# Attention with routed experts on one core: the stretch ahead of the experts reordered, the router placed by two clocks, the second product in row form, four experts' rows turned by VectorE via DRAM

## The chip, the cores and the metric

The kernel runs on one core of one Trainium2 chip. A core has TensorE (PE, matrix products; PEld is its loading of stationary operands), VectorE (DVE), ScalarE (ACT), GpSimd (POOL) and SyncE (SP, which issues DMAs), each with an instruction stream of its own, executed in order, and 16 DMA engines. The metric is the device time of one execution in microseconds (us). It is compared by the median of several runs.

## What is computed

An attention with a sigmoid instead of a softmax, 8 batches of 12 heads, 448 positions, 64 values per head, all in fp32. Its output is read as 3584 tokens of 768 values. Each token goes to exactly one of 8 experts, 448 tokens per expert, assigned greedily by the largest logit over all pairs of token and expert. An expert is a two-layer product with a ReLU between.

```python
scores = scale * np.matmul(q, k.transpose(0, 1, 3, 2)) - np.log(S)
attn = 1.0 / (1.0 + np.exp(-scores))          # x = attn @ v, as (3584, 768)
logits = x @ w_gate                            # (3584, 8)
for idx in np.argsort(-logits.flatten()):      # greedy, with a capacity
    tok, e = idx // E, idx % E
    if assigned[tok] >= 0 or counts[e] >= cap: continue
    assigned[tok] = e; counts[e] += 1
for e in range(E):
    h = np.maximum(x[assigned == e] @ w1[e], 0.0)   # 448x768 @ 768x1024
    out[assigned == e] = h @ w2[e]                  # 448x1024 @ 1024x768
```

## The kernel before

**Precision.** A product of two fp32 operands is made of three products of a faster format: each operand is split into a high part (a rounded copy) and a low part (the difference), and high x high, high x low and low x high are summed in PSUM. For a weight tile `wr`, ACT writes the high part `wh` (L596) and POOL, now and then DVE, the low part `wl` (L598).

**Attention** (about the first 276 us) goes over 48 pairs of heads: `turn`, `scores`, `rest_scores`, `av`. `av` leaves the result transposed, in `XT[b]` with the 768 values along the partitions: a copy by DVE (L469) and, for every second pair, an addition (L471). `logits` (L476) multiplies `XT` by the gate weights; for the last batch it is cut in two, the first four pairs ahead of the last `av` and two behind it.

**Rows to DRAM.** `rows` (L486) turns a block of 112 tokens of `XT` on PE (six transposes, L490), copies it from PSUM with ACT (L492) into one of four buffers `xr`, and SP writes it to `xs` in DRAM (L493). There are 32 such blocks. They are left to the stretch between attention and the experts, mixed into the first search: two after each of its steps.

**The router.** For k = 0 to 7, `phase(k)` finds the expert that fills up next and its list of 448 tokens: `keys` (DVE), `search` (16 steps of two bits of a threshold; each step counts with three DVE instructions, L173), `pick`, `place`, `lists`. In phase 0 the sum over partitions of each step is a small PE matmul (L185); in later phases it is done by DVE alone with 32x32 transposes (L189, L195). `pick`, `place` and `lists` go through PE several times (L224, L252, L257, L284, L291). Each `yield` hands control back with the time, in ns, after which the next piece shall be emitted.

**The experts.** Rows of x are gathered by the list with an indirect DMA of POOL (`gather`, L618), turned on PE (`xturn`: three transposes per half block, L632; ACT takes the high part, L635, DVE the low part, L636). The first product has 4 x 36 matmuls of 448 columns, weights stationary (L680 to L684), into tiles of two PSUM banks. ReLU and split follow (L688 to L692). The second product has 3 x 48 matmuls of 448 columns, weights stationary again (L715 to L719), so its result lies transposed: ACT copies it to `yt` (L723), and `untranspose` turns it back on PE, 12 chores of two transposes per expert (L645), copied by ACT (L650). An indirect DMA of POOL writes the rows to their tokens (L653).

**What sets the order.** The whole program is one hand-made order. `moe` yields after every matmul with an assumed cost (`MM = 189` ns), which drives `clock`. When the clock passes `t_route`, the next piece of the router is emitted, and its yield plus `SLACK` sets the next time. `chores` holds (due time, last expert, piece): gathers, turns, result transposes; one per `CHORE_NS`. At the end of an expert, `flush` emits what the next one still needs, and as long as its list isn't there, the router is run on. `stream` issues weight loads three units ahead (SP, four buffers) and their splits two ahead. The simulated clock only sets the order in the streams; the engines then run as their semaphores let them.

```python
if t >= t_route:
    t_route = t + next(route, 0) + SLACK
```

Of the kernel before, what the change touches and what calls it, by code (L numbers as in the profile page):

```python
# [21 lines left out]
XR_BUFS = 12  # L22
XT_BUFS = 8
XA_BUFS = 4
AT_BUFS = 8
YT_BUFS = 3
LATE_PER_STEP = 2
LATE_KEYS = 2
T_KEYS, T_KE, T_STEP, T_DVE, T_KAP, T_PICK, T_TOT, T_OH, T_BT = 3600, 2100, 2050, 2025, 500, 2600, 600, 3800, 600
SLACK = 150  # L30
# [4 lines left out]
W_DVE = 84  # L35
# [78 lines left out]
class Router:  # L114
# [42 lines left out]
    def search(self, pe):  # L157
# [10 lines left out]
        for st in range(16):  # L168
# [11 lines left out]
            if pe:  # L180
                if nX is not None:
                    nc.vector.tensor_scalar(nX, K.kk[:, st + 1], JP, None, OP.bitwise_xor)
                yield T_STEP
# [30 lines left out]
            if not pe:  # L214
                yield T_DVE
# [31 lines left out]
    def place(self):  # L247
# [7 lines left out]
        yield T_TOT  # L255
# [10 lines left out]
    def lists(self):  # L266
# [6 lines left out]
        rr = wk.tile([112, 32], I16, name="r_rr")  # L273
# [6 lines left out]
        yield T_OH  # L280
# [7 lines left out]
        yield T_BT  # L288
# [30 lines left out]
    def phase(self, k):  # L319
        if k:  # L320
            self.remove()
        if k < 7:
            self.keys()
            yield T_KEYS
            yield from self.search(k == 0)
            yield T_KAP
            self.pick()
        else:
            self.left()
        yield T_PICK  # L330
        yield from self.place()
        yield from self.lists()


def moe_attention(tc, q, k, v, w_gate, w1, w2, out):
# [7 lines left out]
    with contextlib.ExitStack() as ctx:  # L343
# [8 lines left out]
        ld = actx.enter_context(tc.tile_pool(name="ld", bufs=2))  # L352
        wk = actx.enter_context(tc.tile_pool(name="wk", bufs=2))
        xa = actx.enter_context(tc.tile_pool(name="xa", bufs=1))

# [96 lines left out]
        def av(b, pr):  # L452
# [16 lines left out]
            nc.vector.tensor_copy(XT[b][:, pr, :], p[:, :S])  # L469
# [16 lines left out]
        def rows(b, c):  # L486
            xr = xa.tile([CP, DM], F32, name="xr", bufs=XA_BUFS)
# [13 lines left out]
        for i in range(NPR + 1):  # L501
# [32 lines left out]
        ps_t = ctx.enter_context(tc.tile_pool(name="ps_t", bufs=2, space=PSUM))  # L534
        ps_s = ctx.enter_context(tc.tile_pool(name="ps_s", bufs=2, space=PSUM))
        ps_a = ctx.enter_context(tc.tile_pool(name="ps_a", bufs=2, space=PSUM))
        R = Router(tc, K, cp, rw, ps_a)
# [4 lines left out]
        def routing():  # L542
            for kx in range(E):
# [6 lines left out]
                yield 0  # L550
# [11 lines left out]
        actx.close()  # L562

# [4 lines left out]
        units = [(kx, st, i, j) for kx in range(E) for st, n in ((0, 4), (1, 3)) for i in range(n) for j in range(2)]  # L568
# [4 lines left out]
        def load_w(u, behind=False):  # L573
# [5 lines left out]
            t = wp.tile([128, 1024], F32, name="wr")  # L579
            if behind:  # L580
                nc.gpsimd.memset(t[:1, :1], 0.0)
            if st == 0:
                t = t[:, :768].rearrange("p (a f) -> p a f", a=3)
                src = w1[ds(gate[kx], 1)].rearrange("e (a p) f -> p (e a) f", p=128)
                nc.sync.dma_start(t, src[:, 3 * j:3 * j + 3, i * 256:(i + 1) * 256])
            else:
                t = t.rearrange("p (a f) -> p a f", a=4)
                src = w2[ds(gate[kx], 1)].rearrange("e (a p) f -> p (e a) f", p=128)
                nc.sync.dma_start(t, src[:, 4 * j:4 * j + 4, i * 256:(i + 1) * 256])
            raw[u] = t  # L590

        def split_w(u):
            n = 3 if units[u][1] == 0 else 4
            hi = wp.tile([128, 1024], F32R, name="wh")[:, :n * 256].rearrange("p (a f) -> p a f", a=n)
            lo = wp.tile([128, 1024], F32R, name="wl")[:, :n * 256].rearrange("p (a f) -> p a f", a=n)
# [14 lines left out]
        xg, XH = {}, {}  # L610

# [8 lines left out]

        def xturn(kx, j, n, hf, wide):
# [3 lines left out]
            xh, xl = XH[kx]  # L625
            if wide and hf:
# [12 lines left out]
        MM = 189  # L639

        def untranspose(kx, yr, i, yt, j, n, t0=0, end=False):

            p = R.bank() if end and j % 2 else ps_t.tile([128, 512], F32, name="tp")
            for d2 in range(2):
# [171 lines left out]
```

## Time and profile before

| | us |
|---|---|
| median of 3 runs | 891.27 (888.68 to 891.42) |
| the profiled execution | 887.23 |
| its span, first to last instruction | 885.5 |
| attention | 0 to about 276 |
| rows, first search, first list, first turn | about 276 to 335 |
| eight experts | 335 to 877 |
| last writes | 877 to 885.5 |

Times in the views below are microseconds from the span's start. In the chain of waits a row is start, length and what the end of the program hung on there; "issue" means that the engine waited for nothing the profile shows. In the groups a row gives line, engine, operation, out<-in, shape and type, count, then busy time and mean ns of one, then the engine's idle time ahead of it and what ended it. Matmuls are pipelined: the length of one is a latency, and what one costs in a row of them is the distance of their starts. A busy PE is thus not a PE at its peak.

### The profile page before, as it was taken

How to read it: one execution, taken by the hardware profiler on the slowest of the kernel's cores; microseconds unless marked ns; L12 is line 12 of the kernel's file. 1: busy time of each engine (PE TensorE's matmuls, PEld its weight loads, DVE VectorE, ACT ScalarE, POOL GpSimd, SP SyncE). 2: the span in 40 equal slices, each digit the busy share in tenths (PEclk: the TensorE clock that was granted, in tenths of full speed). 3: DMA queues.
4: the chain of work that ended last, by engine and by line, in shares of the span. 5: the costliest groups of instructions: out<-in, count | busy, mean ns of one | idle time of the engine just before them, and what ended most of it. 6: DMA issues, size and time to landing. Idle time of an engine off the chain costs nothing.

```text
span 885.5 us, 16232 instructions
## 1 busy us (share of the span) xinstructions
PE 837.8 (95%) x5507; PEld 639.0 (72%) x5507; DVE 531.4 (60%) x2047; ACT 456.2 (52%) x610; POOL 467.4 (53%) x449
## 2 busy tenths in 40 slices
PE   6999999999998729998999999999999999999996
PEld 3455455455555518987988988988888888889996
DVE  4665555555554778958869779779689521421110
ACT  6777777777774724434424424434434434443431
POOL 9645444444400014846864964873883882752651
PEclk9999999999999969999999999999999999999999
DMA  9876666665603945434443542452552542632511
GB/s 172 168 144 127 132 125 123 131 126 120 138 12 100 299 161 153 136 107 161 136 133 117 146 156 75 157 164 95 153 164 70 178 146 72 228 111 72 192 49 63
DMA packets 203507, 117.57 MB, mean 133 GB/s; under 512 B 143936, under 2 KB 193088, under 8 KB 203424
## 3 DMA queue, kind: packets, MB, share of 16 engines
q1 hardware_dynamic: 190688, 83.03, 36.0%
q0 software_dynamic: 10880, 33.28, 11.9%
q8 instruction: 43, 0.70, 0.3%
q10 hardware_dynamic: 1856, 0.23, 0.2%
q14 instruction: 40, 0.33, 0.1%
HBM read 94.47 MB, written 22.02 MB: 132 GB/s over the span
## 4 chain that ended last, share of the span: by engine, by line
PE 77%; DVE 8%; DMA 5%; issue 4%; POOL 3%; ACT 1%; SPq 1%; POOLq 0%; ACTq 0%; DVEq 0%
PE tp L461 13%; PE sc L437 11%; PE sc L682 8%; PE sc L680 8%; PE sc L684 8%; PE sc L717 6%; PE sc L719 6%; PE sc L715 6%; PE tp L467 2%; DMA xs<-xr 2%; DVE r_junk L173 2%; PE sc L447 2%; PE tp L645 2%; DMA xr<-xs,r_idx 2%; PE tp L632 2%
## 5 line engine op out<-in xcount | busy, mean ns | idle before, releaser
L598 POOL TENSOR_TENSOR wl<-wr,wh 128x768 fp32r<-128x768 f32 (+1 forms) x96 | 205.9, 2155 | 134.6 <-ACT wh L596 126.9
L427 ACT ACTIVATE at<-sc,bias 128x896 f32<-128x896 f32 x168 | 161.0, 1006 | 63.1 <-PE sc L447 38.2
L372 POOL DMA_DIRECT2D nkq<-in_q_dram x188 | 118.6, 646 | 111.5 <-DVE kqT L412 104.7
L719 PE MATMUL sc<-hh,wl 128*128 128x448 f32 (+2 forms) x400 | 151.4, 378 | 0.0
L717 PE MATMUL sc<-hl,wh 128*128 128x448 f32 (+2 forms) x400 | 145.4, 364 | 0.1
L684 PE MATMUL sc<-xh,wl 128*128 128x448 f32 (+2 forms) x396 | 145.4, 367 | 0.0
L682 PE MATMUL sc<-xl,wh 128*128 128x448 f32 (+2 forms) x396 | 144.9, 366 | 0.0
L715 PE MATMUL sc<-hh,wh 128*128 128x448 f32 (+2 forms) x400 | 143.9, 360 | 0.0
L680 PE MATMUL sc<-xh,wh 128*128 128x448 f32 (+2 forms) x396 | 143.8, 363 | 0.0
L173 DVE TENSOR_SCALAR_CACHE_REDUCE r_junk<-r_KE,r_T 128x224 bf16<-128x224 f32 x315 | 123.2, 441 | 0.1
L461 PE MATMUL tp<-at,nv 128*64 128x448 f32 x576 | 118.8, 548 | 0.0
L596 ACT ACTIVATE wh<-wr 128x768 fp32r<-128x768 f32 (+1 forms) x112 | 102.0, 939 | 13.2 <-DMA wr<-in_moe_w_dram 13.1
L692 POOL TENSOR_TENSOR hl<-yt,hh 128x896 fp32r<-128x896 f32 x32 | 68.3, 2136 | 44.5 <-ACT yt L691 41.8
L421 DVE TENSOR_TENSOR kqL<-kqT,kqH 128x896 fp32r<-128x896 f32 (+1 forms) x49 | 52.6, 1073 | 58.3 <-ACT kqH L419 58.2
L688 ACT ACTIVATE hh<-sc 128x896 fp32r<-128x896 f32 x32 | 29.5, 920 | 111.0 <-PE sc L684 111.0
L618 POOL DMA_INDIRECT xr<-xs,r_idx x32 | 32.0, 1002 | 97.5 <-ACT wh L596 86.7
L717 PEld LDWEIGHTS sc<-hl,wh 128*128 128x128 f32 x400 | 75.2, 188 | 7.0 <-issue 1.1
L598 DVE TENSOR_TENSOR wl<-wr,wh 128x768 fp32r<-128x768 f32 (+1 forms) x16 | 25.1, 1571 | 91.7 <-ACT wh L596 91.5
L461 PEld LDWEIGHTS tp<-at,nv 128*64 128x64 f32 x576 | 37.1, 136 | 59.1 <-issue 57.9
L682 PEld LDWEIGHTS sc<-xl,wh 128*128 128x128 f32 x396 | 74.5, 188 | 6.3 <-issue 0.5
L715 PEld LDWEIGHTS sc<-hh,wh 128*128 128x128 f32 x400 | 75.6, 189 | 4.4
L680 PEld LDWEIGHTS sc<-xh,wh 128*128 128x128 f32 x396 | 74.7, 189 | 5.5
(156 smaller groups left out, 1323.7 us busy)
## 6 DMA issues: line engine op xcount, KB each, us to landing
wr<-in_moe_w_dram SPq DMA_DIRECT2D x64, 384.0 KB
wr<-in_moe_w_dram SPq DMA_DIRECT2D x48, 512.0 KB
xs<-xr SPq DMA_DIRECT2D x32, 336.0 KB
nkq<-in_k_dram SPq DMA_DIRECT2D x190, 56.0 KB
nkq<-in_q_dram POOLq DMA_DIRECT2D x188, 56.0 KB, 2.6
nv<-in_v_dram SPq DMA_DIRECT2D x92, 96.0 KB
nr<-in_v_dram SPq DMA_DIRECT2D x46, 32.0 KB
xr<-xs,r_idx POOLq DMA_INDIRECT x32, 4.4
```

What stands on the lines that cost most here:

```text
L173: nc.vector.tensor_scalar(junk, KE, T[:, i:i + 1].bitcast(F32), None, OP.is_ge, OP.add, accum_out=cnt[:, i:i + 1])
L372: qn.dma_start(t[o:o + 32, n], rws[x])
L427: nc.scalar.activation(a, p[:, :, :S], AF.Sigmoid, bias=bias, scale=1 / math.sqrt(D))
L461: nc.tensor.matmul(p[j * 64:j * 64 + 64, :S], nat["v", b, g][:, h0 + j, c, :], AT[b, pr, c][:, j, :], start=(c == 0), stop=(c == 2 and pr ...
L596: nc.scalar.activation(hi, raw[u], AF.Copy)
L598: eng.tensor_tensor(lo, raw[u], hi.bitcast(F32), OP.subtract)
L680: nc.tensor.matmul(ph[:, f, lo:hi], wh[:, a, fs], xh[:, dd, lo:hi], start=st, stop=False)
L682: nc.tensor.matmul(ph[:, f, lo:hi], wh[:, a, fs], xl[:, dd, lo:hi], start=False, stop=False)
L684: nc.tensor.matmul(ph[:, f, lo:hi], wl[:, a, fs], xh[:, dd, lo:hi], start=False, stop=en)
L715: nc.tensor.matmul(py[:, d2, :w], wh[:, a, dsl], h1, start=st, stop=False)
L717: nc.tensor.matmul(py[:, d2, :w], wh[:, a, dsl], h2, start=False, stop=False)
L719: nc.tensor.matmul(py[:, d2, :w], wl[:, a, dsl], h1, start=False, stop=(j == 1 and a == 3))
```

## The change

1. *Stretch ahead of the experts.* The last batch's logits run in one piece behind the last `av`; the copy of that last product goes to ACT, beside DVE's addition. No row block stands ahead of the router's start any more, three follow it ahead of the first search, then two per step as before. The pools of attention are released first, so that the row blocks get eight buffers (`xo`) and three PSUM tiles instead of four and two.
2. *Router by two clocks.* Pieces yield (cost on DVE, whether the next piece needs PE). A second clock `dve` sums DVE's costs, those of the turns of x included; a piece that begins on PE is emitted 150 ns after it, another 400 ns ahead of it. All costs are new, a matmul of the first product counts 206 ns and one of the second 175, and turns and routing matmuls are added to the PE clock. From phase 1 on, an index tile of `lists` lies in PSUM instead of SBUF.
3. *Second product in row form.* Tokens are stationary (128 columns of h, high or low), the weights move, 384 columns at a time: 2 halves x 8 slices x (3 + 3 + 3 + 2) = 176 matmuls per expert, whose result has tokens along the partitions. The last block has 64 tokens: its high and low parts lie side by side as one stationary operand, and the two halves of the result are added (ACT copies and a POOL addition; DVE for the very last). `untranspose` is gone; ACT copies the result straight into `yr`. Weight units of the second product become 8 of 768 values per partition instead of 6 of 1024. The ReLU is written in two parts.
4. *Turn by DVE via DRAM for experts 4 to 7.* After the gather, SP writes the rows to a DRAM buffer `xq` (`stage`) and reads them back with four DMAs per pair of blocks (`fetch`) so that 32x32 block transposes by DVE into PSUM (`vturn`) complete the turn, with the 768 values spread over the partitions in another order. The first weights of these experts are loaded in the matching order, with four DMAs of 32 partitions per unit instead of one.

```diff
@@ search, lists, phase
-            if not pe:
-                yield T_DVE
+            if not pe and st < 15:
+                yield T_STEP if st else T_STEP0, False
...
-        rr = wk.tile([112, 32], I16, name="r_rr")
+        rr = wk.tile([112, 32], I16, name="r_rr") if alone else P[:, 320:352]
...
@@ av, rows and the stretch ahead
-            nc.vector.tensor_copy(XT[b][:, pr, :], p[:, :S])
+            (nc.scalar.copy if (b, pr) == (B - 1, NP - 1) else nc.vector.tensor_copy)(XT[b][:, pr, :], p[:, :S])
...
-            xr = xa.tile([CP, DM], F32, name="xr", bufs=XA_BUFS)
+            xr = xo.tile([CP, DM], F32, name="xr", bufs=XO_BUFS)
...
-            if old == (B - 1, NP - 2):
-                bg.append(lambda: logits(B - 1, range(NP - 2)))
...
-        logits(B - 1, [NP - 2, NP - 1])
-        late.pop(0)()
+        logits(B - 1, range(NP))
...
+        lctx.close()
         ps_a = ctx.enter_context(tc.tile_pool(name="ps_a", bufs=2, space=PSUM))
+        xo = actx.enter_context(tc.tile_pool(name="xo", bufs=1))
+        ps_s = actx.enter_context(tc.tile_pool(name="ps_w", bufs=3, space=PSUM))
         R = Router(tc, K, cp, rw, ps_a)
         R.start(LE)
         late.pop(0)()
...
@@ load_w
+                else:
+                    src = w1[ds(gate[kx], 1)].rearrange("e (g a p) f -> g p (e a) f", g=4, a=ND)
+                    for g in range(4):
+                        nc.sync.dma_start(t[32 * g:32 * g + 32], src[g, :, 3 * j:3 * j + 3, fs])
...
+        def stage(kx, j, n):
+            nc.sync.dma_start(xq[kx % 2][j * 128:j * 128 + n], xg[kx, j][:n])
+
+        def fetch(kx, j0, j1):
+            t = xg[kx, 4 + j0] = xp.tile([128, 8, DM // 4], F32, name="xw", bufs=2)
+            v = xq[kx % 2].rearrange("(j c) (g w) -> g c j w", c=32, g=4)
+            for g in range(4):
+                nc.sync.dma_start(t[32 * g:32 * g + 32, :j1 - j0], v[g, :, j0:j1])
+
+        def vturn(kx, j, n, hf):
...
+            dve[0] = max(dve[0], clock[0]) + T_VTURN
...
+            for a in range(3):
+                nc.vector.transpose(p[:, a * n:(a + 1) * n].rearrange("p (j w) -> p j w", w=32),
+                                    w[:, :, (3 * hf + a) * 32:(3 * hf + a + 1) * 32])
...
+            nc.scalar.activation(xh[sl], pv, AF.Copy)
+            nc.vector.tensor_tensor(xl[sl], pv, xh[sl].bitcast(F32), OP.subtract)
...
@@ moe: ReLU and second product
+                parts = ((h[:, :, 0], h[:, :, 1], slice(0, W2)), (r[:, :, :64], r[:, :, 64:], slice(W2, S)))
+                for h1, h2, t in parts:
+                    nc.scalar.activation(h1, ph[:, :, t], AF.Relu)
...
+            for i in range(2):
+                cs = slice(i * W2, (i + 1) * W2)
+                py = [ps_s.tile([128, 2, 512], F32, name="sc") for _ in range(2)]
+                for j in range(4):
...
+                    for z in range(2):
+                        for a in range(2):
...
+                            for c in range(2):
+                                o = py[z][:, c, :W2]
+                                if z == 0 or c == 0:
+                                    t = slice((2 * z + c) * 128, (2 * z + c + 1) * 128)
+                                    terms = ((h[:, 0, t], wh), (h[:, 1, t], wh), (h[:, 0, t], wl))
+                                else:
+                                    terms = ((r, wh), (r, wl))
+                                for n, (hs, w) in enumerate(terms):
+                                    nc.tensor.matmul(o, hs, w[:, a], start=st and n == 0,
+                                                     stop=en and n == len(terms) - 1)
+                                    yield MM2
...
@@ prepare and the loop
-                lag = max(5000, min(14000, start + 40000 - t0))
+                lag = max(6500, min(17000, start + 50000 - t0))
...
+                if kx + 1 >= BY_DVE:
+                    for j, n in blocks():
+                        t = t0 + 1500 * j + T_LAND
+                        chores.append((t, kx + 1, lambda j=j, n=n: stage(kx + 1, j, n)))
+                        if j % 2:
...
+                            chores.append((t + T_BACK2, kx + 1, lambda r=r: fetch(kx + 1, *r)))
...
-                    t_route = t + next(route, 0) + SLACK
+                    cost, hop = next(route, (0, False))
+                    dve[0] = max(dve[0], t) + cost
+                    clock[0] += T_PE if hopped[0] else 0
+                    hopped[0] = hop
+                    t_route = dve[0] + (T_HOP if hop else T_FEED)
```

The new costs, in ns: `T_KEYS` 4850, `T_STEP0` 3300, `T_STEP` 2340, `T_KAP` 350, `T_PICK` 3000, `T_TOT` 700, `T_OH` 4900, `T_BT` 1500, `T_XL` 560, `T_TURN` 420, `T_PE` 250, `T_LAND` 8000, `T_BACK2` 4000, `T_READ` 5000, `T_VTURN` 1200. `W_DVE` goes from 84 to 96 with the finer units: both mean expert 6, from which on DVE makes every second `wl`.

More of the change, by code (lines that the diff above doesn't have):

```diff
@@ L34 @@
 FIRST = 4000.0
-W_DVE = 84
+BY_DVE = 4
+T_LAND, T_BACK2, T_READ, T_VTURN = 8000, 4000, 5000, 1200
+W_DVE = 96
 class Consts:
@@ L264, in place, with lists @@
         self.sl = sl
-    def lists(self):
+    def lists(self, alone):
         nc, K, wk, sl = self.nc, self.K, self.wk, self.sl
@@ L329, in phase @@
             self.left()
-        yield T_PICK
+        yield T_PICK, True
         yield from self.place()
-        yield from self.lists()
+        yield from self.lists(k == 0)
 def moe_attention(tc, q, k, v, w_gate, w1, w2, out):
@@ L562, in moe_attention @@
         actx.close()
+        ps_t = ctx.enter_context(tc.tile_pool(name="ps_t", bufs=2, space=PSUM))
+        ps_s = ctx.enter_context(tc.tile_pool(name="ps_s", bufs=2, space=PSUM))
         wp = ctx.enter_context(tc.tile_pool(name="wp", bufs=4))
@@ L566, in moe_attention @@
         xp = ctx.enter_context(tc.tile_pool(name="xp", bufs=1))
-        units = [(kx, st, i, j) for kx in range(E) for st, n in ((0, 4), (1, 3)) for i in range(n) for j in range(2)]
+        units = [(kx, st, i, j) for kx in range(E) for st, n in ((0, 4), (1, 2)) for i in range(n) for j in range(8 // n)]
         NU = len(units) // E
@@ L578, in load_w @@
                 gate[kx] = nc.sync.value_load(picked[kx][:1, :1], min_val=0, max_val=E - 1)
-            t = wp.tile([128, 1024], F32, name="wr")
+            t = wp.tile([128, 768], F32, name="wr")
             if behind:
@@ L610, in moe_attention @@
         xg, XH = {}, {}
+        xq = [dr.tile([S, DM], F32, name=f"xq{i}") for i in range(2)]
         def blocks():
@@ L625, in xturn @@
             xh, xl = XH[kx]
+            if not wide:
+                clock[0] += T_TURN
+            dve[0] = max(dve[0], clock[0] + 900) + T_XL
             if wide and hf:
@@ L638, in moe_attention, with scatter @@
         scat, chores = [], []
[L639 to L644, printed above, removed]
-                nc.tensor.transpose(p[:n, d2 * 128:(d2 + 1) * 128], yt[:, d2, j * 128 - t0:j * 128 - t0 + n], ident)
-            dst = yr[j][:n, i * 256:(i + 1) * 256]
-            if end and j % 2:
-                nc.vector.tensor_copy(dst, p[:n, :256])
-            else:
-                nc.scalar.copy(dst, p[:n, :256])
-            if i == 2:
-                nc.gpsimd.memset(spacer, 0.0)
-                ins = nc.gpsimd.indirect_dma_start(
-                    out=out, out_offset=bass.IndirectOffsetOnAxis(ap=listed[kx][:n, j:j + 1], axis=0),
-                    in_=yr[j][:n], in_offset=None)
-                for o in scat:
-                    tc.declare_no_dep(ins.ins, o.ins, reason="rows of other tokens")
-                scat.append(ins)
+        MM, MM2, W2 = 206, 175, 384
+        def scatter(kx, yr, j, n):
+            nc.gpsimd.memset(spacer, 0.0)
+            ins = nc.gpsimd.indirect_dma_start(
+                out=out, out_offset=bass.IndirectOffsetOnAxis(ap=listed[kx][:n, j:j + 1], axis=0),
+                in_=yr[j // 2][:n, j % 2], in_offset=None)
+            for o in scat:
+                tc.declare_no_dep(ins.ins, o.ins, reason="rows of other tokens")
+            scat.append(ins)
         def moe(kx):
@@ L666, in moe @@
                 cuts = ((0, 256), (256, S)) if kx + i == 0 else ((0, S),)
-                mm = 107 if len(cuts) > 1 else MM
+                mm = 117 if len(cuts) > 1 else MM
                 for lo, hi in cuts:
@@ L730, in moe_attention @@
+        clock, dve = [0.0], [FIRST]
         while 0 not in listed:
```

147 lines of the change are left out of this document (79 added, 68 removed).

## The prediction

> **What bounds the kernel now.** I read the page's busy line first, then windows by stage, then the chain of waits between attention and the experts, then the timeline of TensorE (PE) among the experts.
>
> ```profile
> PE 837.8 (95%) x5507; PEld 639.0 (72%) x5507; DVE 531.4 (60%) x2047; ACT 456.2 (52%) x610; POOL 467.4 (53%) x449
> ```
>
> ```profile
> 301.00:305.00 4.00, 3.17 (x26) 2.33 (x23) 2.85 (x19) 2.17 (x3) 0.00 (x0) 1.00 0.95 299
> 581.70:643.60 61.90, 61.60 (x350) 54.00 (x350) 50.15 (x264) 25.43 (x41) 41.07 (x29) 1.00 0.41 131
> ```
>
> A window gives its length, then the busy time of PE, PEld, DVE, ACT and POOL, the granted clock, DMA share and GB/s. Among the experts (second window, from one routing list to the next) PE is full at clock 1.00, and DVE has 11.75 us free. So what is taken off PE there is worth its slot, and nothing else is, as long as DVE keeps up. Ahead of the experts PE isn't full; there the chain decides:
>
> ```profile
> 269.58 0.90 PE tp L482 x32
> 275.18 0.59 PE tp L482 x16
> 277.55 0.66 PE rt L134 x2
> 282.86 0.52 DVE r_junk L173 x3
> 300.67 4.42 DMA xs<-xr
> 306.99 0.81 ACT xr L492
> 315.01 0.18 PE rt L185
> 316.85 0.18 PE rt L185
> 317.51 0.17 DVE r_kap L217
> ```
>
> The chain there is the first routing search: 282.86 to 317.51, 34.65 us for 16 steps, while an unhindered step takes 316.85 - 315.01 = 1.84. The search's small matmuls (L185) queue in PE behind row transposes, those behind ACT's copies into xr, and those behind the write that frees a buffer (300.67). The experts' first matmuls follow at a fixed distance: pick, list, gather, turn of x.
>
> **The stretch ahead.** The logits at 269.58 leave their place between the last two products, so all behind them starts 0.90 earlier. The copy of the last product goes to ACT and runs beside DVE's addition instead of ahead of it: up to 0.7 more. All six pairs' logits then start at 275.18 - 1.6 = 273.6 and take at most 0.90 + 0.59 = 1.5; 0.4 for the sum into LE brings R.start to 275.5. It starts at 277.55 today, behind a row: -2.0. *The search*: eight row buffers instead of four, three PSUM tiles instead of two. Two rows a step cost ACT 2 x 0.81, less than 1.84, and PE isn't full even today (3.17 of 4.00). The writes need 32 x 344 KB / 299 GB/s = 36.8 us, from 277 to about 314: a row comes every 0.93 us and leaves every 1.15, so the backlog reaches eight only near the end. I take 30.5 for the 16 steps (the first is longer): -4.2, together **-6.2**. Bounds: -2 if the writes gate the steps as today, -7.5 if every step takes 1.84. The gather comes some 10 us after the search, with the writes done either way.
>
> **The matmuls of the experts.** Spacing by width, and what an interruption costs (timeline; start, length, instruction):
>
> ```profile
> 346.26 0.37 PE L682 MATMUL sc<-xl,wh 128*128 128x448 f32 x1
> ...
> 367.94 0.37 PE L715 MATMUL sc<-hh,wh 128*128 128x448 f32 x1
> 336.25 0.28 PE L682 MATMUL sc<-xl,wh 128*128 128x256 f32 x1
> ...
> 337.44 0.28 PE L684 MATMUL sc<-xh,wl 128*128 128x256 f32 x1
> 409.73 0.36 PE L682 MATMUL sc<-xl,wh 128*128 128x448 f32 x1
> 409.94 0.38 PE L645 MATMUL tp<-ident,yt 128*128 128x128 f32 x2
> 410.07 0.45 PE L684 MATMUL sc<-xh,wl 128*128 128x448 f32 x1
> 410.36 0.36 PE L680 MATMUL sc<-xh,wh 128*128 128x448 f32 x1
> 464.61 0.36 PE L717 MATMUL sc<-hl,wh 128*128 128x448 f32 x1
> 464.81 0.49 PE L632 MATMUL tp<-ident,xr 128*128 128x128 f32 x3
> 465.06 0.46 PE L719 MATMUL sc<-hh,wl 128*128 128x448 f32 x1
> 465.35 0.37 PE L715 MATMUL sc<-hh,wh 128*128 128x448 f32 x1
> ```
>
> ```profile
> L717 PEld LDWEIGHTS sc<-hl,wh 128*128 128x128 f32 x400 | 75.2, 188 | 7.0 <-issue 1.1
> ```
>
> 448 columns: 21.68 us / 107 = 0.203. 256 columns: 1.19 / 10 = 0.119. On the line through both, 384 columns take 0.203 - 64 x 0.00044 = 0.175.
>
> *Second product*: 144 x 0.203 = 29.2 per expert becomes 2 x 8 x (3+3+3+2) = 176 matmuls of 384 columns, 30.8: +1.57 for seven experts, and +0.2 for the last, whose final third is cut in two today: **+11.2**. From below, 384 scaled straight from 448 (0.174) gives +10. From above, each of these matmuls has its own weight load, and the load's row says 0.188: at that spacing 176 x 0.013 x 8 = 18.3 come on top. I keep 0.175, since the 256-column matmuls have a load each too and run at 0.119. The Trainium skill ("TensorE: Matmul & The Clock Gate", section "LDWEIGHTS (loading the stationary operand)") puts a load at columns / 1.2, for 128 columns an estimate of 107 ns; this sides with the spacing against the load's own row, and by it the term stays +11.2 too.
>
> *Result transposes removed*: two of L645 stretch 409.73 to 410.36, 0.63 for what takes 0.406 alone: 0.224. Of 96 such chores 94 lie inside the matmuls: **-21.1**. Two lie in the tail, whose end is set by four indirect writes in a row on POOL:
>
> ```profile
> 877.14 0.27 PE L719 MATMUL sc<-hh,wl 128*128 128x192 f32 x1
> 880.42 0.91 POOL L653 DMA_INDIRECT out_dram<-xr,r_idx  x1 [0.23 <-issue]
> ```
>
> Today the fourth starts 3.0 us after the last matmul's end at 877.41, with two of the four ahead of that end. After, the first can go once tokens 0 to 255 are copied (0.81 of ACT, 1.75 ahead of the end), and three follow at about 1.3 each: +3.1. **0**.
>
> *Turn of x for experts 4 to 7*: three of L632 stretch 464.61 to 465.35, 0.74 for 0.406: 0.334. 32 such go, -10.7. PE also waits for DVE at some of the 48 among the experts, and two thirds of that go, -2.1; together **-12.8**:
>
> ```profile
> PE tp L632 <- DVE xl L636: 3.2, 5, 0.9
> ```
>
> *First hand-over*:
>
> ```profile
> 391.68 0.16 DVE L293 TENSOR_SCALAR r_idx<-rt 128x4 int32<-128x4 f32 x1 [0.90 <-PE rt L291]
> 401.28 0.36 PE L719 MATMUL sc<-hh,wl 128*128 128x448 f32 x1
> ...
> 408.02 0.47 PE L680 MATMUL sc<-xh,wh 128*128 128x448 f32 x1
> 475.56 0.47 PE L680 MATMUL sc<-xh,wh 128*128 128x448 f32 x1
> ```
>
> Expert 1's list comes at 391.68, some 56 us after the first matmuls (335.3, just ahead of the 256-column rows), so all eight turns stand in a block, 401.28 to 408.02: 6.7 us. Interleaved they cost 8 x 0.334 = 2.7. The new planner counts 206 per matmul beside a real 203 (189 stood there) and sums DVE's costs on a clock of their own: 4.0 + 14 x 2.34 + 2.69 + 3.0 + 0.7 + 4.9 + 1.5 and the hops, so list 1 falls about 50 us after the start: **-4.0** (0 if it stays late).
>
> **What is added to other engines.**
>
> ```profile
> L412 DVE STREAM_TRANSPOSE kqT<-nkq 128x896 f32<-128x896 f32 (+1 forms) x49 | 53.2, 1085 | 8.8 <-DMA nkq<-in_q_dram 4.0 <-DMA nv<-in_v_dram 2.5 <-DMA nkq<-in_k_dram 1.6
> L189 DVE STREAM_TRANSPOSE r_ct<-c_CN 128x32 f32<-128x32 f32 x96 | 20.3, 212 | 3.3
> L636 DVE TENSOR_TENSOR xl<-tp,xh 128x384 fp32r<-128x384 f32 (+1 forms) x60 | 28.7, 501 | 24.5 <-ACT xh L635 24.3
> ```
>
> *DVE turns.* One vturn is three block transposes of 128 columns (no such row; by L412's rate 0.155 each, by L189's floor 0.212), then a copy of 384 columns on ACT (half of L492's 0.81) for which DVE stands still, because its next instruction in order is the 0.50 subtraction: 1.4 to 1.9 with hand-overs, and behind it queue the search steps. I take 1.6, as each hand-over adds some 0.1. Eight are 12.8 where 8 x 0.50 = 4.0 stood, so DVE's busy time rises from 50.15 to 59. Some 5 of today's 11.75 free are waits for PE's small routing matmuls that stay: 64 in all. PE's expert period is 475.56 - 408.02 = 67.5 today; less 2.7 of result transposes and 2.7 of turns, plus 1.6, it is 63.7. The lists of experts 5 and 6 are built beside such turns; they come late by nothing to 5 us each, and PE stands at the routing matmuls, which are placed by the planned 1.2 a turn: **+3** (0 to +10). The Trainium skill ("VectorE: DVE Perf Modes", section "The three transpose paths") speaks against this move: it keeps full 128x128 transposes for TensorE and prices VectorE's block transpose at 311 ns. By that, as an estimate, three transposes take 0.93 and a turn 1.9, and the term goes to its upper end. No row here shows which.
>
> *ACT*: Relu in two parts and the h0 copy, 0.81 + at most 0.4 + 0.95 (0.81 x 896/768), about 2.1 before the second result tile may reuse that bank; its matmuls start 12 x 0.175 = 2.1 later. A tie: **+1** over eight experts (0 to +3). *POOL*: 41.07 of 61.90 today; the same splits in smaller pieces and one addition per half: hidden, as long as it stays under PE's 63.7. *DMA*: 4 x 2.75 MB more, there and back, at a share of 0.41: hidden if in time.
>
> **Sum**, from the profiled execution's 887.23 (span 885.5): -6.2 - 21.1 - 12.8 - 4.0 + 11.2 + 3 + 1 = -28.9, 858.3. The timed runs shown lie higher, at a median of 891.27; with the same difference **862**.
>
> **Rivals.** *DVE sets the pace* (0.20): turns of 1.9 and late reads back, twice 5 us over the taken 3, and expert 6's turns late at its start: +10, 872. For it: 64 against 63.7. Against: the last list needs no search, so the lag ends there.
> *DVE keeps up and the tie is won* (0.15): 858.
> *The weight load paces the row form* (0.05): +18.3, 880. Against it stand the 256-column rows.
> *SP's queue stalls and the kernel gets slower* (0.05):
>
> ```profile
> 765.15 7.14 DMA xr<-xs,r_idx
> 322.71 3.63 DMA wr<-in_moe_w_dram
> ```
>
> The write of x to DRAM waits in SP for its gather, and behind it stand the weights. The plan allows 8 us; POOL may issue the gather 4 us late behind three of its pieces (41.07/29 = 1.4 each), and it lands up to 7.14 after that: SP stands 3 to 4 us, and again for the read back. Cover: three units ahead are 3 x 18 x 0.203 = 11.0, less 3.63 for the load and some 3 for the split on ACT and POOL, 4.4. With some 7 us lost per expert over four experts the gain is gone; at 10 it is 902. Against: the waits of neighbouring blocks overlap.
>
> **Numbers.** Forecast 0.55; these four 0.20, 0.15, 0.05, 0.05. Within 0.3% (2.7 us, about what can't be told from no change) I count 0.01 of the SP case and 0.02 of the DVE and weight-load cases together, slower 0.04, faster 0.93. The range, 850 to 880, takes in below the full front gain and no wait for DVE, above the DVE rival with its bounds and the weight load.
>
> **What would show it.** Right: no L645; 384-column matmuls at 0.175; R.start near 275.5 and a search near 30.5 us; no block of eight turns ahead of expert 1; expert periods near 64, and near 61 for the last two. Wrong: spacing near 0.188; PE waiting for DVE at routing matmuls in experts 3 to 5; weight splits that wait for DMA behind a staged block; turns that end after their expert should start.

## The result, and the profile after

The changed kernel takes a median of 947.66 us (947.15 to 948.41) against 891.35 for the one before (three runs from 888.68 to 891.42, and one of 2087.74 that the ratio leaves out): a ratio of 1.064, 95% interval 1.062 to 1.066. It is slower by 56 us where 29 less were forecast. The profiled execution took 947.15 us, its span is 945.2.

The page's busy line, and the windows that answer to those of before: the stretch ahead, and DVE's time from list 4 to list 5.

```profile
PE 825.0 (87%) x5427; PEld 651.1 (69%) x5427; DVE 568.6 (60%) x2143; ACT 441.2 (47%) x602; POOL 485.3 (51%) x510
```

```profile
301.00:305.00 4.00, 3.36 (x31) 3.01 (x30) 3.66 (x27) 3.27 (x5) 0.00 (x0) 1.00 0.98 341
585.20:672.10 86.90, 68.25 (x381) 64.11 (x381) 62.25 (x288) 27.08 (x44) 49.85 (x39) 0.88 0.48 142
```

In the first window DVE is busy for 3.66 of 4.00 us where it was 2.85: the first search no longer stands behind row transposes. Over the whole span PE is busy 12.8 us less than before, and the span is 59.7 longer: the loss is waiting. A list that took 61.9 takes 86.9 now, and the granted clock in it is 0.88 where it was 1.00. The waits of PE name the place:

```profile
PE sc L712 <- ACT xh L656: 58.2, 3, 20.5
...
PE sc L754 <- ACT wh L605: 6.6, 1, 6.6
```

The 6.6 is a late weight in expert 6, to which run 10 comes back. The three waits at L712 are the first matmuls of experts 4, 5 and 6, which wait for rows turned by DVE (`xh` is ACT's copy of a turn). The timelines of PE and DVE give the way for expert 4: the first matmul of expert 3 and its last one; the list (L295); the first turn (transposes L652, ACT's copy L656, subtraction L657) and the second; the first matmuls of expert 4.

```profile
544.68 0.36 PE L712 MATMUL sc<-xh,wh 128*128 128x448 f32 x1
...
585.21 0.16 DVE L295 TENSOR_SCALAR r_idx<-rt 128x4 int32<-128x4 f32 x1 [1.50 <-PE rt L293]
...
607.44 0.34 PE L754 MATMUL sc<-wl,hr 128*128 128x384 f32 x1
...
610.42 1.04 DVE L652 STREAM_TRANSPOSE tp<-xw 128x128 f32<-128x128 f32 x3
611.49 0.49 ACT L656 ACTIVATE xh<-tp 128x384 fp32r<-128x384 f32 x1 [11.30 <-DVE tp L652]
612.02 0.56 DVE L657 TENSOR_TENSOR xl<-tp,xh 128x384 fp32r<-128x384 f32 x1 [0.56 <-ACT xh L656]
612.49 1.04 DVE L652 STREAM_TRANSPOSE tp<-xw 128x128 f32<-128x128 f32 x3
...
626.43 0.74 PE L712 MATMUL sc<-xh,wh 128*128 128x448 f32 x1 [18.65 <-ACT xh L656]
626.97 0.60 PE L714 MATMUL sc<-xl,wh 128*128 128x448 f32 x1
```

List 4 comes 585.2 - 544.7 = 40.5 us into expert 3, and PE runs out of work at 607.4 + 0.3, 22.5 after it. The first turn begins 25.2 after the list and the last one ends near 628, so PE stands for 18.65. One turn takes 612.49 - 610.42 = 2.07 of DVE, and one search step stands among the eight. Experts 5 and 6 repeat it:

```profile
672.13 0.16 DVE L295 TENSOR_SCALAR r_idx<-rt 128x4 int32<-128x4 f32 x1 [1.49 <-PE rt L293]
...
710.30 0.74 PE L712 MATMUL sc<-xh,wh 128*128 128x448 f32 x1 [19.05 <-ACT xh L656]
...
760.23 0.16 DVE L295 TENSOR_SCALAR r_idx<-rt 128x4 int32<-128x4 f32 x1 [1.48 <-PE rt L293]
...
798.49 0.74 PE L712 MATMUL sc<-xh,wh 128*128 128x448 f32 x1 [20.50 <-ACT xh L656]
```

PE's stand also puts off the small routing matmuls that follow in its stream. Between list 4 and list 5 DVE waits for one of them longer than for anything else (3.5 for the same matmul in the kernel before):

```profile
DVE r_km L229 <- PE rt L226: 10.8, 1, 10.8
```

From list 3 to list 4, without a turn by DVE, the same kernel took 66.3 (list 3 comes at 518.9). Of the 20.6 that come on top, about 7 are this wait; the rest is the turns: DVE is busy for 62.25 where it was 52.18, and waits for ACT's copies. So the next list comes later in its expert and the wait repeats: list 5 comes 45.7 into expert 4, list 6 49.9 into expert 5.

The parts without a turn by DVE are near the forecast. Expert 7, with nothing in between, gives the spacings (first and last start of each kind), and the chain of waits gives the first and the last of the four writes at the end:

```profile
876.05 0.36 PE L712 MATMUL sc<-xh,wh 128*128 128x448 f32 x1
...
905.60 0.37 PE L716 MATMUL sc<-xh,wl 128*128 128x448 f32 x1
905.81 0.51 PE L754 MATMUL sc<-wh,hb 128*128 128x384 f32 x2
...
936.21 0.34 PE L754 MATMUL sc<-wl,hr 128*128 128x384 f32 x1
```

```profile
935.93 0.98 POOL out_dram L685
...
939.75 0.91 POOL out_dram L685
```

384 columns: (936.21 - 905.81) / 175 = 0.174. 448 columns: (905.60 - 876.05) / 143 = 0.207, where 0.203 stood; the last part comes back to it. The first of the last four writes goes ahead of the last matmul's start, the fourth 3.2 behind its end at 936.55, as the prediction has it.

### The profile page after: what moved, and what is told of

The parts are those of the page before. It is cut to its first block, busy times and chain, and to the rows that moved or that the text cites. A ratio compares the mean times of both kernels' runs of the same rounds, so it can differ in the third digit from the quotient of the medians.

```text
span 945.2 us, 16768 instructions
## 1 busy us (share of the span) xinstructions
PE 825.0 (87%) x5427; PEld 651.1 (69%) x5427; DVE 568.6 (60%) x2143; ACT 441.2 (47%) x602; POOL 485.3 (51%) x510
## 5 line engine op out<-in xcount | busy, mean ns | idle before, releaser
L607 POOL TENSOR_TENSOR wl<-wr,wh 128x768 fp32r<-128x768 f32 x110 | 201.4, 1849 | 76.0 <-ACT wh L605 65.1
L754 PE MATMUL sc<-wh,hb 128*128 128x384 f32 x768 | 203.1, 343 | 7.8 <-ACT wh L605 6.6
L712 PE MATMUL sc<-xh,wh 128*128 128x448 f32 (+2 forms) x396 | 147.6, 373 | 58.2 <-ACT xh L656 58.2
L754 PEld LDWEIGHTS sc<-wh,hb 128*128 128x128 f32 x768 | 139.4, 190 | 10.6 <-ACT wh L605 7.0
L605 ACT ACTIVATE wh<-wr 128x768 fp32r<-128x768 f32 x128 | 103.5, 849 | 88.8 <-DMA wr<-in_moe_w_dram 41.8
L754 PE MATMUL sc<-wl,hb 128*128 128x384 f32 x384 | 131.4, 342 | 2.3 <-POOL wl L607 2.3
L712 PEld LDWEIGHTS sc<-xh,wh 128*128 128x128 f32 x396 | 77.2, 195 | 65.8 <-ACT xh L656 59.2
L728 POOL TENSOR_TENSOR hb<-h,hb 128x768 fp32r<-128x768 f32 x32 | 59.2, 1849 | 65.5 <-ACT h L725 65.5
L722 ACT ACTIVATE hb<-sc 128x768 fp32r<-128x768 f32 x32 | 26.0, 812 | 135.7 <-PE sc L716 135.7
L716 PEld LDWEIGHTS sc<-xh,wl 128*128 128x128 f32 x396 | 76.9, 194 | 8.1 <-POOL wl L607 1.1
L607 DVE TENSOR_TENSOR wl<-wr,wh 128x768 fp32r<-128x768 f32 x18 | 23.4, 1303 | 92.8 <-ACT wh L605 84.1
L754 PEld LDWEIGHTS sc<-wl,hb 128*128 128x128 f32 x384 | 73.0, 190 | 3.7 <-POOL wl L607 2.8
```

The costliest lines, as they stand in the source:

```text
L605: nc.scalar.activation(hi, raw[u], AF.Copy)
L607: eng.tensor_tensor(lo, raw[u], hi.bitcast(F32), OP.subtract)
L712: nc.tensor.matmul(ph[:, f, lo:hi], wh[:, a, fs], xh[:, dd, lo:hi], start=st, stop=False)
L716: nc.tensor.matmul(ph[:, f, lo:hi], wl[:, a, fs], xh[:, dd, lo:hi], start=False, stop=en)
L728: nc.gpsimd.tensor_tensor(h2, h0[:, :, t], h1.bitcast(F32), OP.subtract)
L754: nc.tensor.matmul(o, hs, w[:, a], start=st and n == 0, stop=en and n == len(terms) - 1)
```

## The experiments

Line numbers shift by a few between these kernels; the names of the tiles are the same. Where no interval is given, one execution was timed; executions of one kernel lie up to 5 us apart (run 4: 880.62 to 885.84).

**1. Without the turns by DVE** (all eight experts turned by PE; the loading order of the weights goes back with it).

```diff
-BY_DVE = 4
+BY_DVE = 8
```

> The changed kernel with all experts' rows turned by TensorE (no write to DRAM, no read back, no block transposes, the first weights in one DMA per unit). Theory 1: the turn via DRAM is the whole loss, because the list falls some 40 us into an expert of 62 and the chain gather, write, read back, turn takes 41 more. Then the waits of 19 to 21 us ahead of experts 4, 5 and 6 go (58), the 17 us that expert 6 loses to late weights go, and 4 us of slow clock behind the waits; 32 turns of 0.33 us on TensorE come back, with waits for VectorE 11 to 30 us: 880 to 897 from 947. Theory 2: row form or the new planner cost the time; then it stays above 915.

Measured 895.68, ratio 1.0049 (1.0032 to 1.0065), as theory 1 expects. So the DVE turns cost 52 us, and what is left is still slower than before. PE's waits among experts 1 to 6 show a place:

```profile
PE tp L673 <- DVE xl L677: 15.7, 12, 2.6
```

**2. Old placement of the router on top of it.**

```diff
-                    dve[0] = max(dve[0], t) + cost
-                    clock[0] += T_PE if hopped[0] else 0
-                    t_route = dve[0] + (T_HOP if hop else T_FEED)
+                    t_route = t + cost + SLACK
...
-        MM, MM2, W2 = 206, 175, 384
+        MM, MM2, W2 = 189, 163, 384
```

and the old costs of the pieces, the old `lag` of the turns, `T_TURN` and `T_PE` 0.

> As noturn (all turns on TensorE), with the router placed as in the kernel before: its costs, 150 ns of slack, one clock, and the same assumed rate per column. So front and row form alone are changed against the kernel before. Theory 1: in experts 1 and 2 of the changed kernel TensorE loses 4.7 us each at the turns to VectorE, since the new planner leaves VectorE no slack and the subtraction waits behind search steps; the old placement has slack, so 868 to 876 (887 - 6.2 - 21.1 + 11.2 = 871 by the prediction's terms). Rival: the placement doesn't matter, within 3 us of noturn.

Measured 879.54, ratio 0.9867 (0.9843 to 0.9891): faster than both kernels. It missed its expectation by 4 us; the distance to the kernel before, 1.3%, is clear of the noise. The two clocks thus cost 16.1. The row of the waits in the same window:

```profile
PE tp L674 <- DVE xl L678: 2.1, 3, 1.0
```

**3. The stretch ahead alone**, on the kernel before.

```diff
-            xr = xa.tile([CP, DM], F32, name="xr", bufs=XA_BUFS)
+            xr = xo.tile([CP, DM], F32, name="xr", bufs=XO_BUFS)
...
-        logits(B - 1, [NP - 2, NP - 1])
+        logits(B - 1, range(NP))
```

and the rest of part 1.

> The kernel before with the new stretch ahead of the experts alone (row buffers, logits earlier, three PSUM tiles, the last product's copy on ACT); row form, planner's clocks and DVE turns as before. If the front's gain passes to the end unchanged, the first expert matmul starts some 6.3 us earlier (about 329) and so does everything behind it: 883 to 887. If the lists of the experts, which DVE builds without a pause, set the experts' pace already, less of it arrives: 888 to 891. What lies between this run and the one with row form and the old placement (879.5) is then the row form's own gain: 4 to 8 us by the first theory, about 10 by the second; the prediction's terms for it (second product +11.2, transposes -21.1) said -9.9.

Measured 884.62 (ratio 0.9931, 0.9908 to 0.9954), and the first matmul of expert 0 at 329.36 in its trace: 6 us (4 to 8 by the interval), passed on to the end. Between it and run 2 lie 0.64% of 891, 5.7 us, for the row form with the old placement (the interval is about 3 to either side).

**4. The turns' distance**, on run 1.

```diff
-CHORE_NS = 1000
+CHORE_NS = 1700
```

> All eight experts' rows turned by TensorE, the new two clocks kept, and only the least distance between two planned chores raised from 1000 to 1700 ns. Theory 1 (turns are emitted about 1.03 us apart because the planner's time stamp does not see its own addition of 420 for a turn, while DVE in order frees a PSUM tile only every 1.6 us): the waits of the turns for DVE's subtraction fall from 15.7 us in experts 1 to 6 to under 5, and the time from 895.7 to 880 to 886. Theory 2 (DVE has no room among the experts, and the turns wait whatever their distance, or the loss lies in phases planned too long): the time stays at 893 to 898.

Measured 881.17, ratio 0.991 (0.9876 to 0.9943): 14.5 of the 16.1 come back with one number, though 6.5 of the wait stays where under 5 was expected. PE's timeline in run 1 shows how every second turn waits; behind it stands the row of the waits, as above, of run 4:

```profile
530.58 0.55 PE L673 MATMUL tp<-ident,xr 128*128 128x128 f32 x3 [2.63 <-DVE xl L677]
531.66 0.49 PE L673 MATMUL tp<-ident,xr 128*128 128x128 f32 x3
533.83 0.55 PE L673 MATMUL tp<-ident,xr 128*128 128x128 f32 x3 [0.98 <-DVE xl L677]
534.92 0.49 PE L673 MATMUL tp<-ident,xr 128*128 128x128 f32 x3
```

```profile
PE tp L673 <- DVE xl L677: 6.5, 11, 1.2
```

Turns leave in pairs 1.08 apart, while DVE frees two PSUM tiles in 534.92 - 531.66 = 3.26 (a search step and two subtractions). `t_chore = t + CHORE_NS` takes `t` from ahead of the 420 ns that the turn adds to the clock. These rows account for 9.2 of the 14.5; the rest was not located.

**5. No write to DRAM.** The DVE turns read fixed rows, and the first turn is planned 6.5 us after the list, where the change has 18.5 (`T_LAND`, `T_BACK2`, `T_READ` and 1.5 for the second block of a pair).

```diff
-T_LAND, T_BACK2, T_READ, T_VTURN = 8000, 4000, 5000, 1200
+T_LAND, T_BACK2, T_READ, T_VTURN = 0, 0, 5000, 1200
...
-            v = xq[kx % 2].rearrange("(j c) (g w) -> g c j w", c=32, g=4)
+            v = xs[kx * S:(kx + 1) * S].rearrange("(j c) (g w) -> g c j w", c=32, g=4)
```

> The changed kernel, but the read back takes fixed rows of xs, so that it waits for no gather and no write (the write to DRAM is left out, and the turned rows are not those of the list); block transposes begin 12 us earlier in the plan. Theory 1 (length of the chain): the waits ahead of experts 4, 5 and 6 shrink from 19 to 21 us to 5 to 9 each and expert 6 gets its weights in time: about 890 to 900. Theory 2 (VectorE's own time for eight turns, 16.6 us, on top of the search): waits of 15 us and more stay, above 920.

Measured 908.45: between the two theories, 12.8 above run 1.

**6. The same, at the planned times of the change** (12 us later).

```diff
-T_LAND, T_BACK2, T_READ, T_VTURN = 0, 0, 5000, 1200
+T_LAND, T_BACK2, T_READ, T_VTURN = 8000, 4000, 5000, 1200
```

> The run with DVE turns that reads fixed rows instead of writing the gathered ones to DRAM (908.45; the write is left out and the turned rows of experts 4 to 7 are not the list's), but with the turns at the planned times of the change again: 12 us later than in that run. Nothing is written to DRAM, SP waits for no gather, and DVE does the same work. Theory 1 (what the way costs is its length: the turns end later than the expert should start, since lists 4 to 6 stand 40 us and more into the expert before): PE waits some 15 to 20 us ahead of each of experts 4, 5 and 6 again, 930 to 945. Theory 2 (the write, the waits in SP's queue behind it and the weights that come late are what the way costs): 905 to 918.

Measured 937.11, and the waits of PE in this run, beside those of run 5 below it:

```profile
PE sc L712 <- ACT xh L656: 55.5, 3, 20.8
```

```profile
PE sc L712 <- ACT yr L760: 23.2, 3, 11.5
```

Nothing is written to DRAM here, and PE waits as in the change. The lateness comes from the place of the turns in DVE's stream: 18.5 us planned ahead of the first one, behind a list with only 22.5 left. In run 5 the last to end was a copy of results on ACT (`yr`), which stands behind the copies of the turns in ACT's stream.

**7. The way through DRAM alone**: writes and reads for experts 4 to 7 as in the change, rows turned by PE. The first weights of these experts keep the change's order of rows, which the rows of x do not have then, so their products are of unmatched rows.

```diff
-                                chores.append((t + T_BACK2 + T_READ + 1000 * i, kx + 1,
-                                               lambda ...: vturn(kx + 1, jj, n, hf)))
...
-                    return
```

> The new kernel with the writes to DRAM and the strided reads back for experts 4 to 7 where the change has them, but the rows turned by TensorE as for experts 1 to 3 (what is read back is used by nothing). Against the run without DVE turns (895.7), where the change itself (947.7) adds 52. Theory 1 (SP's queue: weights late behind writes that wait for their gathers): most of the 52 is here too, 920 to 940. Theory 2 (the length of the way from list to turned rows, and DVE's own time): only expert 6 loses, as the run with one such expert lost 9: 900 to 912.

Measured 899.93: 4.2 above run 1, at the lower edge of theory 2. From expert 3 on SP stands for 28.3 in all at writes that wait for a gather (60.7 in the change), so such a stall costs little; the stall of the change's size was not run alone, but run 6, without any write, loses 41 of the 52.

**8. DVE's time alone**, on run 1. The planner counts 1.2 us for such a turn, as in the change.

```diff
+            if kx >= 4:
+                jt = xp.tile([128, 128], F32, name="jt", bufs=1)
+                for _ in range(5):
+                    nc.vector.transpose(jt, ident)
```

> The kernel without DVE turns, with five block transposes of 128x128 into a spare tile ahead of each subtraction of experts 4 to 7: about the time on DVE that a DVE turn has more than a TensorE turn (some 13 us for each expert), without the way through DRAM and without a wait of the rows for it. Theory 1 (DVE's own time sets the pace of the lists): the phases of lists 5 and 6 grow from 67 to 77 or more and the experts wait: 908 to 925. Theory 2 (what costs is the way; a DVE phase of 77 alone eats only the distance between the last list and its use): phases near 77, but 896 to 905.

Measured 922.47, 26.8 above run 1. Windows from list 4 to list 5, and the added instruction in the view of its line (min/median/max in ns):

```profile
586.20:668.00 81.80, 72.12 (x391) 65.55 (x392) 64.52 (x305) 27.11 (x44) 47.94 (x38) 0.92 0.37 114
```

```profile
L670 DVE STREAM_TRANSPOSE jt<-ident x160: 289/311/314, 600.3 to 814.0; 128x128 f32<-128x128 f32 x160
```

DVE is busy for 64.52 and the phase takes 81.8, so 17 us of idle remain beside the added load. Here PE's own turns stand behind it: from the first expert on they wait 33.1 for DVE, 18.7 in run 1.

**9. Earlier lists**: run 2 with the DVE turns of the change.

```diff
-BY_DVE = 8
+BY_DVE = 4
```

> Old placement of the routing steps with the row form, and the rows of the last four experts turned by DVE through DRAM as in the change. Theory 1 (what cost most was where the list stood: list 4 came 40.5 us into expert 3 and the way from it to the turns takes 41): list 4 comes at about 571, 32 us into expert 3, so the first wait ahead of expert 4 is about 5 us instead of 19, later ones some 5 us longer each because a phase grows by DVE's 12 us for the turns, and expert 6 keeps its late weights: 900 to 915, that is 20 to 35 above the run without DVE turns (879.5). Theory 2 (DVE's turns cost the same wherever the list stands, through DVE's own time and the way through SP): 52 above it, as between the change and the run without DVE turns: 927 to 935.

Measured 932.06, 52.5 above run 2: the number of theory 2, and my own first theory fell. List 4 does come at 570.4, 32 into expert 3, yet PE waits 15.9 ahead of expert 4: the turns stand between search steps now and end 47 after the list, and PE, which has no turns of its own to make there, arrives 31 after it and not 36. No later expert waits for its rows. The starts of experts 4 and 5, the list between them and the one after (window below: list 5 at 645.2), and what PE waits for from here on:

```profile
617.89 0.74 PE L713 MATMUL sc<-xh,wh 128*128 128x448 f32 x1 [15.93 <-ACT yr L761]
...
696.52 0.40 PE L713 MATMUL sc<-xh,wh 128*128 128x448 f32 x1
...
721.72 0.16 DVE L296 TENSOR_SCALAR r_idx<-rt 128x4 int32<-128x4 f32 x1 [0.93 <-PE rt L294]
```

```profile
PE sc L755 <- ACT yr L761: 12.7, 2, 7.1
PE sc L755 <- ACT wh L606: 6.8, 2, 5.1
PE sc L755 <- ACT h L726: 5.7, 1, 5.7
```

```profile
761.09 0.33 ACT L657 ACTIVATE xh<-tp 128x192 fp32r<-128x192 f32 x1 [1.38 <-DVE tp L653]
761.31 0.79 ACT L761 COPY yr<-sc 128x768 f32<-128x768 f32 x1
```

List 5 comes 27.3 into expert 4, list 6 25.2 into expert 5, each earlier than the 32 of list 4, so DVE's chain of lists is not what holds the experts back here: PE takes 78.6 from expert 4 to expert 5 while the lists are 74.8 apart. PE stands for 25.2 inside the experts at results, weight splits and ReLUs on ACT, which wait in ACT's stream behind the copies of the turns, and those wait for DVE; the last view is ACT just ahead of the end of the longest of these waits. Theory 2 named DVE's time and SP, not ACT. The early lists together with a copy on DVE (runs 11 and 12) were not run, so how much of the 52.5 hangs on ACT's order stays open.

Windows of run 9 from list 4 to list 5, and of run 2 (without DVE turns) for the list before; then the first and the last of the six rows that hold all DVE waited for in that stretch of run 2:

```profile
570.40:645.20 74.80, 58.76 (x329) 54.40 (x328) 59.72 (x289) 24.23 (x40) 42.19 (x34) 0.89 0.51 149
```

```profile
510.60:571.20 60.60, 59.51 (x345) 53.94 (x346) 50.67 (x265) 23.06 (x39) 42.17 (x34) 1.00 0.44 137
```

```profile
DVE r_km L230 <- PE rt L227: 2.5, 1, 2.5
...
DVE r_KE L168 <- PE rt L165: 0.6, 1, 0.6
```

This tight phase of 60.6 has DVE busy for 50.67 and idle for 9.9; 6.7 of these (the six rows together) are round trips to PE, and the rest is spread over the gaps between 265 instructions. With DVE turns none of it is filled: the phase is 74.8 and DVE idle for 15.1 of it, 4.6 of these for ACT's copies. PE's period in run 2 is about 67.

**10. One expert's turns by DVE** (expert 7, the last list, with no search beside it).

```diff
-BY_DVE = 4
+BY_DVE = 7
```

> The changed kernel with only expert 7 turned by VectorE; its list comes a whole expert ahead. Theory 1a: no wait at the boundary of expert 7, but the write to DRAM stands in SP's queue ahead of expert 6's weights until its gather has landed, so expert 6 loses 5 to 17 us: noturn plus 2 to 14. Rival: the queue does no harm where no list is late; noturn minus 3 to 6 us, as 8 turns leave TensorE.

Measured 904.83: 9.1 above run 1, inside what was expected, with no wait at the start of expert 7. But SP waits for a gather for only 3.1 us in this stretch, so its queue was not the cause. ACT's timeline and the row of PE's waits show where expert 6 loses it:

```profile
792.52 0.49 ACT L656 ACTIVATE xh<-tp 128x384 fp32r<-128x384 f32 x1 [1.58 <-DVE tp L652]
792.90 0.81 ACT L722 ACTIVATE hb<-sc 128x768 fp32r<-128x768 f32 x1
...
794.55 0.86 ACT L605 ACTIVATE wh<-wr 128x768 fp32r<-128x768 f32 x1
```

```profile
PE sc L754 <- ACT wh L605: 5.3, 1, 5.3
```

The copies of the turns wait for DVE in ACT's stream, and the ReLU and the weight split of expert 6 stand behind them.

**11 and 12. That copy on DVE**, in run 10 and in the change.

```diff
-            nc.scalar.activation(xh[sl], pv, AF.Copy)
+            nc.vector.tensor_copy(xh[sl], pv)
```

> The run that turns expert 7 alone on DVE (904.83, 9.1 above the run without DVE turns), with the high part xh of a DVE turn copied by DVE instead of ACT; DVE stood still for that copy anyway. Theory 1 (expert 6 loses because ACT's copies of the turns wait for DVE in ACT's stream and the weight splits and ReLUs of expert 6 stand behind them): the wait for wh (5.3) goes, and the time falls to 896 to 900. Theory 2 (SP's queue: weights behind the writes and reads of the rows): it stays at 902 to 907.

> The change (947.7) with the high part of every DVE turn copied by DVE instead of ACT. Theory 1 as above: expert 6 loses 6 to 10 less, the waits ahead of experts 4 to 6 stay near 19 to 21 each, since they are set by the place of the lists and the length of the way: 937 to 942. Theory 2: 944 to 950.

Measured 898.22 and 938.90: both as theory 1 has it, 6.6 and 8.8 less. In run 11 a part of the wait has only moved, to the weight splits that DVE makes for expert 6:

```profile
PE sc L754 <- DVE wl L607: 7.3, 1, 7.3
```

## Why the prediction was wrong

**The whole sum.** The runs split the 56 us into parts, each with the others around it: the stretch ahead -6.2 (run 3), the row form -5.7 (run 2 against 3), the two clocks +16.1 (run 1 against 2), the DVE turns +52.0 (the change against run 1); together +56.2. The first two have an interval of 2 to 3 us to either side. The forecast had -6.2, -8.9 (with the tie on ACT), -4.0 and -9.8.

**The stretch ahead** was right, in its steps too: the router starts at 275.19 where 275.5 stood, the search takes 310.55 - 280.26 = 30.29 where 30.5 stood, the first matmul comes at 329.0, 329.1 by the prediction's terms, and the end moved by the same amount.

**The second product** was right in each price looked at: 0.174 against 0.175, no trace of a weight load that paces (0.05, gone), the transposes gone, the tail 8.6 where 8.1 stood. The first product, which it left alone, has 0.203 per matmul in experts 0, 1, 4, 5 and 6 of the change and 0.207 in experts 2, 3 and 7: 3 x 144 x 0.004 = 1.7 us. The row form as such is not the cause, because run 3, without it, has (363.80 - 341.67) / 107 = 0.207 in its expert 0; the cause stays open.

```profile
341.67 0.39 PE L681 MATMUL sc<-xh,wh 128*128 128x448 f32 x1
...
363.80 0.37 PE L685 MATMUL sc<-xh,wl 128*128 128x448 f32 x1
```

**The first hand-over** failed in its sum for list 1: about 50 us after the start, measured 387.88 - 328.95 = 59:

```profile
387.88 0.16 DVE L295 TENSOR_SCALAR r_idx<-rt 128x4 int32<-128x4 f32 x1 [1.49 <-PE rt L293]
```

By the code, the sum left out that the second clock counts the turns of expert 0 too, 8 x 0.56 as planned, and the jumps of `max(dve, t)` ahead of each piece; what each gave was not measured. With the old placement (run 2) list 1 comes 385.40 - 329.22 = 56 after the start, so the two clocks made it later, not earlier. Two of the eight turns went between matmuls; six stay in a block from 396.2 to expert 1's first matmul at 402.7, with waits for DVE in it, so about 0 came instead of -4.0:

```profile
397.75 1.01 PE L673 MATMUL tp<-ident,xr 128*128 128x128 f32 x6 [1.53 <-DVE xl L677]
```

**The two clocks** stood in the prediction only as the reason for an early list. That they place the *turns* differently was not priced: 420 more on the clock for a turn, and a due time that doesn't see them, so the distance shrank below what two PSUM tiles and a DVE in order allow (run 4). That is 14.5 of the 16.1.

**The turns by DVE** are the step that decided. Its term was +3 (0 to +10) beside -12.8, and four things in it failed. Of the expert periods that were to be near 64, experts 3 to 6 have 81.8, 83.9, 88.2 and 77.6; expert 7, with no turn beside it, takes 60.5 where 61 stood.

*The room on DVE.* "DVE has 11.75 us free", of which "some 5" were to stay. Nearly all of it stays: 9.9 in a tight phase. Then 50.15 busy was to become 59 with the waits for ACT in it; in run 9 it is 59.7 without them, and they are another 0.56 per turn, by the rows of the first one. So the phase is 74.8 instead of 64, longer than PE's 67: with such turns DVE can't keep up, and the rival's +10 was too low. That DVE's chain alone sets the pace is not shown, since in run 9 PE is slower still and waits for ACT. Runs 5 and 8 price DVE's time at 13 and 27 us, each with the waits of ACT or PE behind it.

*One turn.* 2.07 against 1.6 (1.4 to 1.9): a block transpose of 128 columns takes 1.04 / 3 = 0.35 here, outside 0.155 to 0.212. The prediction's own two rows held the answer, 0.212 for 32 columns and 1.085 for 896, but it scaled one by columns and took the other as a floor. A fixed part and a price per column both show in them: on the line through both, 128 columns take 0.309. The Trainium skill ("VectorE: DVE Perf Modes", section "The three transpose paths") has 311 ns for 128x128 in bf16; the trace agrees for fp32, with 311 as the median of run 8. By that page the turn was 1.9. It was weighed, and set aside.

*The way from list to turned rows.* The largest part, and no term had it. The prediction asked whether lists 5 and 6 come late by 0 to 5 us, never how long the way is (18.5 us planned and 25.2 taken to the first turn, 17.9 for the eight and the step among them) against what is left of the expert when the list comes (22.5). For a turn by PE that rest had been enough. List 4 itself, at 40.5 into expert 3, was not worked out. "Turns that end after their expert should start" stood among what would make it wrong, without a price. From run 1, DVE turns with rows at hand cost +12.8 (run 5), their planned lateness +28.7 more (run 6), the real write and what hangs on it +10.5 (the change). Moving list 4 to 8.5 us earlier in its expert cured none of the total (run 9): the wait for rows ahead of expert 4 fell only to 15.9, and in place of the later ones PE waits for ACT behind the copies of the turns.

*What queues behind.* The prediction named the search steps behind a turn on DVE. It did not name ACT's stream, where the copy waits 1.58 for each turn with ReLUs and weight splits behind it: 8.8 us in the change (run 12), and waits of 25.2 in run 9.

**The SP rival** gave the right side, with the wrong mechanism. Around expert 6 SP does stand for 17.0 at a write that waits for its gather:

```profile
SPq L633 <- DMA xr<-xs,r_idx: 22.2, 2, 17.0
```

But with all writes and reads in place and PE turning, the kernel loses 4.2 in all (run 7), not 7 per expert.

**The clock.** Matmuls behind such a wait are slow: the first two of expert 4 stand 626.97 - 626.43 = 0.54 apart, and the granted clock of its first 4.7 us is 0.50:

```profile
626.43:631.10 4.67, 4.67 (x13) 4.10 (x14) 4.06 (x22) 1.79 (x3) 2.25 (x3) 0.50 0.00 0
```

Its first product takes 31.5 us, where 144 x 0.203 are 29.2. The window with the list has a granted clock of 0.88. The Trainium skill ("TensorE: Matmul & The Clock Gate", section "What's actually happening") has TensorE fall to half its clock after an idle window of about 3.4 us; waits of 19 with a granted clock of 0.50 behind them agree with it. At some 2.3 us for each of the three waits it is a small part.

**The version that is faster** is run 2: the new stretch ahead and the row form, with the old placement and PE's turns, 879.54.

## What to carry to other kernels

Idle time of an engine in a busy window isn't room for more work on its chain: look at what each gap waits for, and at the shortest period that the engine has ever shown, before placing anything on it. When work moves to a longer way, compare the way's length with the time left between its trigger and its use; a stall of the main engine then delays the next trigger as well, and repeats. For each instruction that is moved, name what stands behind it on every engine it passes through, the one that only copies included.

## What the runs showed of the hardware that was not expected

- An fp32 block transpose on DVE over 128 partitions took 0.212 us for 32 columns, 0.311 for 128 (median of run 8) and 1.085 for 896: by these rows about 0.18 us for the instruction and 1.0 ns for each column. In a row they are a little farther apart: three of 128 columns into PSUM take 1.04 us, 0.35 each.
- With 384 columns and a new stationary operand for each, matmuls keep a distance of 0.174 us; with 448 columns it is 0.203 in some experts and 0.207 in others of one execution, with the same instructions.
- After a wait of 18.65 us the granted clock of TensorE was 0.50 for 4.7 us.
